# Grouped-query attention on one core: in the one load queue, K of a step behind V of two steps back, V singly

## The chip, the cores and the metric

The kernel runs on one core of one Trainium2 chip. The metric is the device time of one execution in microseconds (us), lower being better. A core has several engines that each take their own instruction stream in order: TensorE (PE, the matmuls; PEld is its loading of the stationary operand), VectorE (DVE), ScalarE (ACT), GpSimd (POOL) and SyncE (SP), which here does nothing but issue data transfers (DMAs). Engines tell each other by semaphores when a piece of work is done, and a DMA raises a semaphore when it has landed.

## What is computed

Two independent problems, A and B, of the same shapes; their results are put side by side in the output. Of each:

```python
# x [16, 80, 576], k_cache and v_cache [16, 16, 512, 128], wq [576, 4096], wo [4096, 576], all bf16
q = (x @ wq).reshape(B, Sq, Hq, Dh).transpose(0, 2, 1, 3)       # 32 query heads of 128
k = jnp.repeat(k_cache, rep, axis=1)                            # 16 KV heads, each for rep = 2 query heads
v = jnp.repeat(v_cache, rep, axis=1)
scores = jnp.einsum("bhqd,bhkd->bhqk", q, k) * (Dh ** -0.5)
p = softmax(scores, axis=-1)
o = jnp.einsum("bhqk,bhkd->bhqd", p, v)
return o.transpose(0, 2, 1, 3).reshape(B, Sq, Hq * Dh) @ wo
```

## The kernel before

**Tiling.** The attention goes in 128 steps `U`, 64 for each problem. A step is one batch element with four KV heads (so eight query heads): its K is one tile of 128 x 4 x 512 bf16 (512 KB), its V another. Eight steps with the same four heads form an octet; for an octet the queries are projected first (`qp`, line 599, and the copy out of PSUM, 615 and 617). Per step, with keys on the partitions:

- 16 score blocks of 128 keys by 160 (two heads of 80 queries), line 714. They run through all steps in groups of three, `qk0`, `qk1`, ..., so that group `t` holds blocks 3t to 3t + 2, and step `U` begins with block 16U.
- For each group the maximum of every row over its three blocks (line 720, DVE) and the exponential (line 724, ACT).
- As every row of a group has a maximum of its own, V's rows have to be scaled to make up for it: a common minimum (744, 747, 751), weights `wt` (754, ACT), and on POOL a cast (757, `wc`) and six multiplications of V by the weights (775, `vs`), whose result is `vp`.
- The products with `vp`: four of four matmuls (`pv`, line 800) and the rest of the queries for a pair of steps (`pr`, 819); then the division by the sums (836, 841, 846), the transposes (863) and their copies (875, 877).

The output projection (`op`, 968) follows in pieces of 16 matmuls, over half the heads at a time; its sums stay in `acc` and go out through four buffers `osb` (996, stores 1002).

PE takes the scores of a step some two steps ahead of its products, so K of a step is used about two steps ahead of V of the same step.

**Buffers.** `kT` has five buffers for K (`NK`), `v_sb` four for V (`NV`). K of step `U` may be loaded when the scores of step `U - 5` are done, V of step `U` when POOL has done the six multiplications of step `U - 4`; both are semaphore waits of SP.

**The queue.** Nearly all loads and the stores are issued by SP, in one order. K is loaded by a transposing DMA (`ldk`, line 682), V by a plain copy (`ldv`, 686); between them stand the pieces of wq (570, 573), wo (645), the transposed x of problem B (537) and the stores (1002). SP issues them strictly in order: while one waits for its buffer, all behind it wait.

**The planner.** The orders of all engines are made while the program is built. `_Sched` is told every operation with a key (where it would stand), what it reads and writes, an assumed duration and a stream, walks through an assumed time and gives each engine the operation that is ready and has the lowest key. `after` names a mark (a number, where mark 4U + u is the product `pv` of step U, head u, or the name of an operation): the operation isn't placed before that one has been. It is a matter of the order alone; at run time there are only the semaphore waits that follow from `reads` and `writes`. What the lines touched by the change do before:

- `KPH = 35`, `KU0 = 10`: from step 10 on, K of step `U` is placed after mark 4U - 35.
- `KRD`: from step 10 on K goes in pairs: that of an even step also waits for the buffer of the next one (resource `kd`, written by every score group).
- `VPH = 16`, `VU0 = 14`: from step 14 on V is placed 2 us (`VLAG`) after mark 4U - 16, the first product of step U - 4.
- `VRD`: from step 14 on V goes in pairs: that of an even step also waits for the buffer of the next one (resource `vd`, written by the last multiplication of every step).
- `VPE`: V of steps 4, 5, 6 and 7 is placed after marks 8, 11, 14 and 17.

The order that comes out in the middle, for instance: K 26, K 27, V 24, V 25, K 28, K 29, V 26, V 27, with weights and stores between.

Of the kernel before, what the change touches and what calls it, by code (L numbers as in the profile page):

```python
# [14 lines left out]
NV = 4  # L15
# [7 lines left out]
VK = 14.0  # L23
# [18 lines left out]
FKEY = dict([(n_, i_ - 100.0) for i_, n_ in enumerate(FIRST)] + [(n_, 0.05 * i_ - 0.49) for i_, n_ in enumerate(LATER)])  # L42
LAND = dict(x00=4.1, w00=6.4, x01=8.0, w01=9.6, k0=11.5, w10=14.5, k1=16.0, v0=18.3, k2=20.5, v1=22.5, k3=25.2, k4=28.0, v2=30.5, k5=33.8, x10=35.4, x11=36.4, w11=39.0, v3=40.6, k6=43.2)
# [5 lines left out]
VENG = "sp"  # L49
# [1 line left out]
VLAG = 2.0  # L51
VPH = 16
VU0 = 14
VPE = {4: 8, 5: 11, 6: 14, 7: 17}
KPH = 35
KU0 = 10
KLAG = 0.0
# [6 lines left out]
NVS = 4  # L64
# [302 lines left out]
def bass_concat_heads__gqa_block_cached__gqa_block_cached__near_ridge_kernel(  # L367
# [18 lines left out]
    NSU = 2 * UPR  # L386
# [8 lines left out]
    with ExitStack() as es:  # L395
# [9 lines left out]
        vp = sb("vp", [128, NVP, 18, VW], BF16)  # L405
# [31 lines left out]
        S = _Sched()  # L437

        def R(res, ver):
            return (res, ver)  # L440
# [37 lines left out]
        def em_warmend(e):  # L478
# [5 lines left out]
              stream="warmset")  # L484
# [12 lines left out]
        for half in range(NPP):  # L497
            x_ap = probs[0][0]
            for part, (k0, k1) in enumerate(XP):
                def em_ldx(e, x_ap=x_ap, half=half, k0=k0, k1=k1):  # L500
# [5 lines left out]
                      writes=[R(("xs", half * NRT + k_), 0) for k_ in range(k0, k1)], dsem="d_x%d%d" % (half, part), land=LAND["x%d%d" % (half, part)],  # L506
                      name="ldx%d.%d" % (half, part), stream="first", dur=0.5, cost=XC * (k1 - k0))
            for blk in range(NRT):
# [11 lines left out]
                def em_xev(e, en=None, half=half, blk=blk, vb=vb):  # L520
# [4 lines left out]
                      stream="X", dur=_mm(5, 128), lat=0.2, alloc=[vb])  # L525
                S.add(("act", "dve") if half else "act" if blk in (1, 3) else "dve", x + 0.3, em_xev, reads=[R(vb, 0)], writes=[R(("xT", half, blk), 0)],
                      name="xev%d" % rb, stream="xed" if half else "xea" if rb in (1, 3) else "xev",
                      dur=dict(act=0.52, dve=0.40), lat=0.13)

        for half in range(NPP):  # L530
            x_ap = probs[1][0]
            st0 = UPR + 16 * half - lead[NG // 2 + 2 * half]
            for ck in range(5):
                def em_ldxt(e, x_ap=x_ap, half=half, ck=ck):
# [6 lines left out]
                      writes=[R(("xT", half, b_), 1) for b_ in range(NRT)] if ck == 0 else [R(("xT", half, "t", ck), 1)],  # L541
                      dsem="d_x%d0" % half, name="ldxt%d.%d" % (half, ck), stream="x", dur=0.7, cost=0.85, xp=True,
                      after=int(4 * (st0 + XR[half][0] + XR[half][1] * ck)))
# [5 lines left out]
        for goct in range(NG):  # L549
# [6 lines left out]
            for pi, (c0, c1) in enumerate(pieces):  # L556
# [10 lines left out]
                for j, (k0, k1, n0, n1) in enumerate(parts):  # L567
                    def em_ldw(e, wq_ap=wq_ap, q=q, wsl=wsl, n0=n0, n1=n1, k0=k0, k1=k1):
                        if k0 == 4:
# [7 lines left out]
                          writes=[R(("wq", wsl, w_, p_), wv) for w_ in range(k0, k1) for p_ in range(n0 // 256, n1 // 256)],  # L577
                          dsem="d_we%d_%d_%d" % (goct, pi, j) if goct < 2 else "%s_%d" % (dsem, j),
                          name="ldw%d.%d.%d.%d" % (goct, pi, k0, n0), stream="wqa" if not goct + pi + j else strm if goct < 2 or k0 < 4 else "wqb", dur=0.5,
                          cost=((0.12 + 0.8 * WQC) * (k1 - k0) / 4.0 if k0 < 4 else 0.4) * (n1 - n0) / 1024.0 * (1.0 if goct < 2 or k0 == 4 else 0.96),  # L580
                          after=int(4 * (sp_ + at)) if goct > 1 else None,
                          lag=WLAG if goct > 1 else 0.0,
                          land=LAND["w%d%d" % (goct, pi)] if goct < 2 else 0.0)

            for i in range(8):
                for c in range(2):
# [34 lines left out]
                    if prob:  # L621
                        xr += [R(("xT", half, "t", ck), 1) for ck in range(1, 5)]
                    S.add("pe", x, em_qp,
                          reads=[R(("wq", wsl, w_, i // 2), wv) for w_ in range(5)] + [R(("wqz",), 0)] + xr,
                          writes=[R(vb, 0)] + [R(("qT", qpos(goct, bl), i), goct) for bl in range(b0, b0 + nb)],
                          name="qp%d.%d.%d" % (goct, i, c), stream="Q" if goct else "Q0",
                          dur=_mm(5, n1 - n0), lat=0.2, alloc=[vb])
                    S.add(("act", "dve"), x + 0.4, em_qev, reads=[R(vb, 0)],
                          writes=[R(("qT", qpos(goct, bl), i), goct) for bl in range(b0, b0 + nb)],
                          name="qev%d.%d.%d" % (goct, i, c), stream="qev" if goct else "qev0",  # L630
                          dur=QEV[n1 - n0] if qpos(goct, b0) + nb <= NQS else QEV[n1 - n0, 2])

        for sg in range(2 * NPAIR):
# [4 lines left out]
            for n in range(2 * NWC):  # L638
# [4 lines left out]
                def em_ldwo(e, wo_ap=wo_ap, h0=h0, hc=hc, wc=wc, c3=c3):  # L643
# [7 lines left out]
                      writes=[R(("wo", c3, wc), sg)]  # L651
                      + ([R(("warm",), 3 + c3), R(("ones",), 1 + c3)] if sg == 0 and wc == 0 else []),
                      dsem="d_wo%d" % c3, name="ldwo%d.%d.%d" % (sg, c3, wc), stream="wo", dur=0.5, cost=WOC,
                      after=int(4 * (base + w0 + ws_ * wc)), lag=WLAG)
# [2 lines left out]
        NT = (NBK + 2) // 3  # L657
        PT0 = [16 * U // 3 for U in range(NSU)]

        def VRD(U):  # L660
            if U < VU0 or U % 2 or U + 1 >= NSU:
                return []
            return [R(("vd", U + 1 - NV), 0)]

        def KRD(U):
            if U < KU0 or U % 2 or U + 1 >= NSU:
# [6 lines left out]
        for U in range(NSU):  # L673
            goct, bl = divmod(U, 8)
            prob, q, half = unit(goct)
            b = half * 8 + bl
            _, kc_ap, vc_ap, _, _ = probs[prob]
            ks, vs = U % NK, U % NV

            def em_ldk(e, kc_ap=kc_ap, b=b, q=q, ks=ks):  # L680
                src = kc_ap[b, 4 * q:4 * q + 4, :, :].rearrange("g (p j) d -> (g p) j d", j=4)
                return e.dma_start_transpose(kT[:, ks, :, :], src)

            def em_ldv(e, vc_ap=vc_ap, b=b, q=q, vs=vs):
                src = vc_ap[b, 4 * q:4 * q + 4, :, :].rearrange("g (p j) d -> p g (j d)", j=4)
                return e.dma_start(v_sb[:, vs, :, :], src)

            S.add("sp", FKEY["k%d" % U] if U < NFK else 5.0 * U - LA - KK, em_ldk, reads=KRD(U), writes=[R(("kT", ks), U)],
                  dsem="d_k%d" % ks, name="ldk%d" % U, stream="K" if U >= NFK else "first", dur=1.8, cost=KC, xp=True,
                  after=4 * U - KPH if U >= KU0 else None, lag=KLAG if U >= KU0 else 0.0, land=LAND.get("k%d" % U, 0.0))  # L690
            S.add(VENG if U >= NVS else "sp", FKEY["v%d" % U] if U < NVS else 5.0 * U - VK, em_ldv, reads=VRD(U),
                  writes=[R(("V", vs), U)],
                  dsem="d_v%d" % vs, name="ldv%d" % U, stream="V" if U >= NVS else "first", dur=VDUR, cost=VC,
                  lag=VLAG if U >= NVS else 0.0, after=VAF[U] if U < 4 else 4 * U - VPH if U >= VU0 else VPE.get(U),
                  land=LAND.get("v%d" % U, 0.0))

        for t in range(NT):
            blks = []
            for B_ in range(3 * t, min(3 * t + 3, NBK)):
                U, r_ = divmod(B_, 16)  # L700
# [22 lines left out]
            def em_exp(e, vb=vb, si=si, sl=sl, n=n):  # L723
# [5 lines left out]
                  name="max%d" % t, stream="max", dur=0.045 + n * 0.00108, lat=0.12, ahead=MXO)  # L729
            S.add("act", kq(t) + 1.1, em_exp, reads=[R(vb, 0), R(("nm", si), t)], writes=[R(("P", sl), t)],  # L730
                  name="exp%d" % t, stream="exp", dur=0.045 + n * 0.00106, lat=0.2)

        for U in range(NSU):
            goct, bl = divmod(U, 8)
            prob, q, half = unit(goct)
            vr, vs, gs = U % NV, U % NVP, U % 2
# [19 lines left out]
            def em_wc(e, gs=gs, vs=vs):  # L756
# [4 lines left out]
                  writes=[R(("gm", gs), U)], name="g%d" % U, stream="g", dur=0.07, lat=0.13, ahead=RCO)  # L761
            S.add("pe", kg + 1.1, em_mb, reads=[R(("gm", gs), U), IDENT], writes=[R(vbx, 0)], name="mb%d" % U,
                  stream="G", dur=_mm(1, 128), lat=0.2, alloc=[vbx], ahead=RCO)
# [3 lines left out]
                  writes=[R(("w", gs), U)], name="w%d" % U, stream="w", dur=0.195, lat=0.15, ahead=RCO + 2.0)  # L767
            S.add("pool", kg + 1.45, em_wc, reads=[R(("w", gs), U)], writes=[R(("vp", vs, "c"), U)], name="wc%d" % U,
                  stream="vs", dur=0.167, lat=0.1)
            for r in range(6):  # L770
                p0, p1 = max(3 * r, off), min(3 * r + 3, off + 16)

                def em_vs(e, p0=p0, p1=p1, vr=vr, vs=vs, off=off, gs=gs, r=r):
                    src = v_sb[:, vr, :, :].rearrange("p g (j d) -> p (g j) d", d=128)[:, p0 - off:p1 - off, :]
                    return e.tensor_scalar(vp[:, vs, p0:p1, 0:128], src, wt[:, gs, r:r + 1], 1.0,  # L775
                                           op0=AluOpType.mult, op1=AluOpType.mult)

                S.add("pool", kg + 1.5 + 0.5 * r, em_vs, reads=[R(("w", gs), U), R(("V", vr), U)],
                      writes=[R(("vp", vs, r), U)] + ([R(("vd", U), 0)] if r == 5 else []), name="vs%d.%d" % (U, r), stream="vs",
                      dur=0.241 + 0.107 * (p1 - p0), lat=0.1)  # L780

            if U % 2 == 0:
# [9 lines left out]
            for u in range(4):  # L792
# [3 lines left out]
                def em_pv(e, u=u, vo=vo, c0=c0, vs=vs, where=where):  # L796
# [10 lines left out]
                    reads=[R(("P", (t0 + r_) % NPS), t0 + r_) for r_ in rs_] + [R(("vp", vs, r_), U) for r_ in rs_ + ["c"]],  # L807
# [23 lines left out]
            for h_, (a_, b_, xo) in enumerate(((0, 3, 2.5), (3, 6, 6.5), (6, 8, 8.5), (8, 10, 9.2))):  # L831
# [6 lines left out]
                def em_on(e, en, pi=pi, vo=vo, a_=a_, b_=b_):  # L838
# [6 lines left out]
                    for k in range(a_, b_):  # L845
# [5 lines left out]
                      stream="rcp", dur=0.08, lat=0.13, ahead=RCO)  # L851
# [364 lines left out]
```

## Time and profile before

| | us |
|---|---|
| three runs: median (lowest to highest) | 721.7 (720.84 to 724.67) |
| the profiled execution: its own time | 718.9 |
| the profiled execution: its span, first to last instruction | 717.1 |

TensorE's granted clock was 0.997 over that execution. All the views that follow are of it; its times are counted from the start of the span. A row of a group reads: line, engine, operation, tile written <- tiles read, shapes, count | busy us, mean ns of one | idle us of the engine just before them, and what ended it. A row of a wait reads: who <- whom: us in total, times, longest us. A row of the timeline reads: start us, us, engine, line, operation, tiles, count [idle us before <- what ended it]. SP's rows (SPq) tell how long it was held by an issue; when a DMA landed is told apart, as "DMA to landing", counted from the start of its issue.

### The profile page before, as it was taken

The page shows a single profiled execution, that of the slowest core. Times are in us where ns is not written, and L with a number is a line of the kernel's source. Part 1 is how long each engine was busy: PE and PEld are TensorE (multiplying, and loading weights), DVE is VectorE, ACT ScalarE, POOL GpSimd, SP SyncE. Part 2 cuts the span into 40 slices and gives each one's busy share as a digit, 9 for nine tenths or more (in the row PEclk, how much of TensorE's full clock was granted, in tenths as well). Part 3 has the DMA queues.
Part 4 walks back from the last instruction along what each step waited for, and adds up shares of the span by engine and source line. Part 5 has one row for each costly group of instructions (what it writes and reads, how often), then busy time and mean ns, then how long its engine had stood idle before and what let it go on. Part 6 is the DMA issues. An engine that isn't in the chain of part 4 may idle for free.

```text
span 717.1 us, 23699 instructions
## 1 busy us (share of the span) xinstructions
PE 696.7 (97%) x9533; PEld 582.2 (81%) x9533; DVE 625.7 (87%) x1605; ACT 588.7 (82%) x1307; POOL 432.5 (60%) x904
## 2 busy tenths in 40 slices
PE   8989999999999999999999999999899999999997
PEld 5658888888888888777888888888788888888885
DVE  5979999998898998988899899899799989999982
ACT  2868988799999899778879888888888889988960
POOL 1546766657567665747556666666566575757570
PEclk9999999999999999999999999999999999999999
DMA  9999999999999999999999999999999988999921
GB/s 234 238 228 259 236 227 261 236 217 244 227 220 232 232 238 245 235 248 230 232 233 225 219 247 234 255 252 211 242 226 208 217 207 226 251 222 241 221 77 33
DMA packets 371028, 160.77 MB, mean 224 GB/s; under 512 B 276832, under 2 KB 367456, under 8 KB 370912
## 3 DMA queue, kind: packets, MB, share of 16 engines
q1 hardware_dynamic: 370832, 159.12, 102.4%
q8 instruction: 77, 1.26, 0.7%
q14 instruction: 39, 0.32, 0.2%
q10 hardware_dynamic: 80, 0.07, 0.0%
HBM read 87.46 MB, written 2.95 MB: 126 GB/s over the span
## 4 chain that ended last, share of the span: by engine, by line
PE 72%; DVE 8%; DMA 8%; POOL 6%; ACT 5%; issue 1%; SPq 1%
PE ps L599 18%; PE ps L968 18%; PE ps L714 14%; PE ps L800 12%; DMA v_sb<-in_A_v_cache_dram 6%; POOL vp L775 6%; DVE negmax L720 5%; PE ps L863 4%; PE ps L819 4%; ACT p_sb L724 3%; DMA v_sb<-in_B_v_cache_dram 1%; PE ps L747 1%; DVE qT L617 1%; PE ps L471 1%; ACT o_sb L846 1%
## 5 line engine op out<-in xcount | busy, mean ns | idle before, releaser
L724 ACT ACTIVATE p_sb<-ps,negmax 128x480 bf16<-128x480 f32 (+1 forms) x683 | 427.3, 679 | 55.0 <-DVE negmax L720 51.3
L775 POOL TENSOR_SCALAR vp<-v_sb,wt 128x384 bf16<-128x384 bf16 (+2 forms) x768 | 407.8, 552 | 41.0 <-DMA v_sb<-in_A_v_cache_dram 32.8
L720 DVE TENSOR_REDUCE negmax<-ps 128x1 f32<-128x480 f32 (+1 forms) x683 | 418.4, 647 | 13.1 <-PE ps L714 11.9
L714 PE MATMUL ps<-qT,kT 128*128 128x160 bf16 x2048 | 233.0, 232 | 1.1 <-ACT p_sb L724 0.7
L599 PE MATMUL ps<-xT,wq_sb 128*128 128x320 bf16 (+2 forms) x1280 | 213.6, 300 | 1.2 <-DVE xT L521 0.6
L800 PE MATMUL ps<-vp,p_sb 128*128 128x129 bf16 x2048 | 195.0, 221 | 10.5 <-POOL vp L775 8.1
L714 PEld LDWEIGHTS ps<-qT,kT 128*128 128x128 bf16 x2048 | 154.1, 97 | 19.1 <-ACT p_sb L724 2.9
L757 POOL CAST vp<-wt 128x18 bf16<-128x18 f32 x128 | 33.8, 264 | 222.8 <-ACT wt L754 222.4
L800 PEld LDWEIGHTS ps<-vp,p_sb 128*128 128x128 bf16 x2048 | 141.8, 98 | 22.5 <-issue 3.6
L599 PEld LDWEIGHTS ps<-xT,wq_sb 128*128 128x128 bf16 x1280 | 115.6, 98 | 35.7 <-DVE wo_sb L479 1.1
L968 PE MATMUL ps<-wo_sb,oTe 128*128 128x288 bf16 x640 | 91.5, 286 | 0.3 <-DVE gmn L751 0.3
L968 PE MATMUL ps<-wo_sb,oTo 128*128 128x288 bf16 x640 | 91.5, 286 | 0.0
L846 ACT ACTIVATE o_sb<-ps,rinv 128x128 bf16<-128x128 f32 x255 | 77.8, 393 | 4.7 <-DVE rinv L836 3.8
L841 DVE TENSOR_TENSOR o_sb<-ps,rinv 128x384 bf16<-128x384 f32 (+1 forms) x155 | 74.7, 484 | 2.0
L617 DVE TENSOR_SCALAR qT<-ps 128x320 bf16<-128x320 f32 (+2 forms) x125 | 59.7, 480 | 16.2 <-PE ps L599 15.7
L968 PEld LDWEIGHTS ps<-wo_sb,oTo 128*128 128x128 bf16 x640 | 60.6, 98 | 13.8
L968 PEld LDWEIGHTS ps<-wo_sb,oTe 128*128 128x128 bf16 x640 | 59.8, 98 | 13.7 <-DVE gmn L751 0.7
L615 ACT ACTIVATE qT<-ps 128x320 bf16<-128x320 f32 (+1 forms) x131 | 57.9, 443 | 12.2 <-PE ps L599 12.1
L863 PE MATMUL ps<-ident,o_sb 128*128 128x128 bf16 x640 | 49.0, 220 | 0.0
L836 DVE RECIPROCAL rinv<-ps 128x3 f32<-128x3 f32 (+1 forms) x256 | 41.1, 167 | 9.0 <-PE ps L819 5.7
L754 ACT ACTIVATE wt<-negmax,gmn 128x6 f32<-128x6 f32 x128 | 40.9, 320 | 7.8 <-DVE gmn L751 7.3
L751 DVE TENSOR_REDUCE gmn<-ps 128x1 f32<-128x128 f32 x128 | 36.4, 284 | 9.4 <-PE ps L747 9.3
(37 smaller groups left out, 310.4 us busy)
## 6 DMA issues: line engine op xcount, KB each, us to landing
v_sb<-in_A_v_cache_dram SPq DMA_DIRECT2D x64, 512.0 KB, 5.3
v_sb<-in_B_v_cache_dram SPq DMA_DIRECT2D x64, 512.0 KB, 5.4
wo_sb<-in_A_wo_dram SPq DMA_DIRECT2D x16, 288.0 KB, 5.9
wo_sb<-in_B_wo_dram SPq DMA_DIRECT2D x16, 288.0 KB, 6.1
wq_sb<-in_B_wq_dram SPq DMA_DIRECT2D x16, 256.0 KB, 4.8
out_dram<-osb SPq DMA_DIRECT2D x40, 72.0 KB, 4.0
wq_sb<-in_A_wq_dram SPq DMA_DIRECT2D x4, 512.0 KB, 5.2
wq_sb<-in_A_wq_dram SPq DMA_DIRECT2D x8, 256.0 KB, 5.5
```

The source lines that it names most:

```text
L599: last = e.matmul(ps[:, vb.phys, 0:n1 - n0], lhsT=wq_sb[:, wsl, ck, i * 128:(i + 1) * 128], rhs=xT[:, half, ck, n0:n1], start=(ck == 0), s ...
L615: r_ = e.activation(dst, src[:, s0:s0 + n_, :], AF.Identity, scale=SCALE)
L617: r_ = e.tensor_scalar(dst, src[:, s0:s0 + n_, :], SCALE, None, op0=AluOpType.mult)
L714: last = e.matmul(ps[:, vb.phys, i * 160:(i + 1) * 160], lhsT=kT[:, U % NK, j, u * 128:(u + 1) * 128], rhs=qT[:, qpos(U // 8, U % 8), u * ...
L720: return e.tensor_reduce(negmax[:, si:si + 1], ps[:, vb.phys, 0:n], axis=AX.X, op=AluOpType.max, negate=True)
L724: return e.activation(p_sb[:, sl, 0:n], ps[:, vb.phys, 0:n], AF.Exp, bias=negmax[:, si:si + 1], scale=1.0)
L775: return e.tensor_scalar(vp[:, vs, p0:p1, 0:128], src, wt[:, gs, r:r + 1], 1.0, op0=AluOpType.mult, op1=AluOpType.mult)
L800: last = e.matmul(ps[:, vo.phys, c0:c0 + 129], lhsT=p_sb[:, sl, i * 160:i * 160 + 128], rhs=vp[:, vs, p_, 0:129], start=(j == 0), stop=(j ...
L841: return e.tensor_tensor(o_sb[:, pi % NOS, a_:b_, :], src[:, :, 0:128], rinv[:, pi % NRI, a_:b_].unsqueeze(2).broadcast_to([128, b_ - a_, ...
L846: last = e.activation(o_sb[:, pi % NOS, k, :], src[:, k - a_, 0:128], AF.Identity, scale=rinv[:, pi % NRI, k:k + 1])
L863: last = e.transpose(dst, o_sb[:, pi % NOS, 4 * h2 + k if k < 4 else 8 + h2, :], ident[:])
L968: last = e.matmul(ps[:, vb.phys, 0:DC], lhsT=lhsT, rhs=wo_sb[:, hi, c3 * DC:(c3 + 1) * DC], start=(hi == 0), stop=(hi == HH - 1))
```

## The change

`VPE` is emptied. `VRD` and the resource `vd` go, so that every V waits for its own buffer only. `KAF` takes the place of the mark for K: from step 6 on K of step `U` is placed after V of step U - 2; from step 10 on the two of a pair are both placed after V of the step before the pair, that is, an even K after V of step U - 1 and an odd one after V of step U - 2. `KRD` stays. `VPH` and `VLAG` stay for V from step 14 on.

```diff
-VPE = {4: 8, 5: 11, 6: 14, 7: 17}
+VPE = {}
...
-        def VRD(U):
-            if U < VU0 or U % 2 or U + 1 >= NSU:
-                return []
-            return [R(("vd", U + 1 - NV), 0)]
+        def KAF(U):
+            if U < 6:
+                return None
+            return "ldv%d" % min(U - 2 + (U >= KU0 and U % 2 == 0), NSU - 1)
...
             S.add("sp", FKEY["k%d" % U] if U < NFK else 5.0 * U - LA - KK, em_ldk, reads=KRD(U), writes=[R(("kT", ks), U)],
                   dsem="d_k%d" % ks, name="ldk%d" % U, stream="K" if U >= NFK else "first", dur=1.8, cost=KC, xp=True,
-                  after=4 * U - KPH if U >= KU0 else None, lag=KLAG if U >= KU0 else 0.0, land=LAND.get("k%d" % U, 0.0))
-            S.add(VENG if U >= NVS else "sp", FKEY["v%d" % U] if U < NVS else 5.0 * U - VK, em_ldv, reads=VRD(U),
+                  after=KAF(U), lag=0.0, land=LAND.get("k%d" % U, 0.0))
+            S.add(VENG if U >= NVS else "sp", FKEY["v%d" % U] if U < NVS else 5.0 * U - VK, em_ldv,
                   writes=[R(("V", vs), U)],
...
-                      writes=[R(("vp", vs, r), U)] + ([R(("vd", U), 0)] if r == 5 else []), name="vs%d.%d" % (U, r), stream="vs",
+                      writes=[R(("vp", vs, r), U)], name="vs%d.%d" % (U, r), stream="vs",
```

The order that comes out for the steps above: V 24, V 25, K 26, K 27, V 26, V 27, K 28, K 29, each V with a wait of its own. In the start-up: V 3, V 4, K 6, V 5, K 7, V 6, K 8, V 7, K 9, V 8, V 9, K 10, K 11 (before: V 3, K 6, K 7, K 8, V 4, K 9, V 5, V 6, V 7, V 8, K 10, V 9, K 11). On POOL the order is the same as before; on PE, DVE and ACT it differs at one place, where the chain of the minimum and the weights of step 18 (744, 747, 751, 754) stands behind one more output projection piece (16 matmuls of line 968) and the two instructions of a query projection and a score group have changed places.

## Prediction

> **What bounds the kernel now.** I read the page first: TensorE (PE) is busy almost throughout, so only its idle time, 717.1 - 696.7 = 20.4 us, is to be had from a change of order.
>
> ```profile
> span 717.1 us, 23699 instructions
> PE 696.7 (97%) x9533; PEld 582.2 (81%) x9533; DVE 625.7 (87%) x1605; ACT 588.7 (82%) x1307; POOL 432.5 (60%) x904
> DMA  9999999999999999999999999999999988999921
> ```
>
> The third row says that the DMA engines are occupied to the end of the loads: a transfer that goes earlier pushes another back. Next, the stretches: where is PE idle?
>
> ```profile
> 0.00:60.00 60.00, 53.60 (x547) 37.89 (x548) 43.81 (x106) 35.21 (x71) 22.77 (x50) 0.97 1.06 243
> 95.00:165.00 70.00, 69.21 (x971) 58.06 (x972) 64.91 (x167) 60.02 (x135) 45.76 (x96) 1.00 1.10 244
> 270.00:375.00 105.00, 100.81 (x1384) 84.80 (x1382) 93.00 (x239) 85.60 (x184) 64.09 (x133) 1.00 1.15 236
> 440.00:512.00 72.00, 69.45 (x980) 58.62 (x979) 61.87 (x160) 62.13 (x142) 45.59 (x95) 1.00 1.08 236
> 512.00:690.00 178.00, 177.32 (x2508) 151.60 (x2506) 164.53 (x426) 157.57 (x352) 114.67 (x240) 1.00 1.00 220
> ```
>
> The columns are the stretch, its length, the busy us of PE, PEld, DVE, ACT and POOL, granted clock, DMA share, GB/s. PE idles 6.4 us in the first 60, 0.8, 4.2 and 2.6 in the next three, and 0.7 in the last, where the DMA engines moved 220 GB/s instead of 236 to 244. The last is loose; the three before it I call crowded. Next, who PE waits for, over the whole span (first row) and in the stretches (0 to 60, 60 to 270, 270 to 375, 440 to 512):
>
> ```profile
> L800 PE MATMUL ps<-vp,p_sb 128*128 128x129 bf16 x2048 | 195.0, 221 | 10.5 <-POOL vp L775 8.1 <-ACT p_sb L724 2.1
> POOL vp L775 <- DMA v_sb<-in_A_v_cache_dram: 32.8, 14, 6.5
> PE ps L800 <- POOL vp L775: 2.9, 1, 2.9
> PE ps L800 <- POOL vp L775: 0.7, 2, 0.4
> PE ps L800 <- POOL vp L775: 3.9, 6, 1.4
> PE ps L800 <- POOL vp L775: 0.6, 1, 0.6
> PE ps L800 <- ACT p_sb L724: 1.9, 1, 1.9
> 505.99 3.18 POOL L775 TENSOR_SCALAR vp<-v_sb,wt 128x384 bf16<-128x384 bf16 x6 [2.85 <-DMA v_sb<-in_B_v_cache_dram]
> 507.28 0.39 PE L800 MATMUL ps<-vp,p_sb 128*128 128x129 bf16 x4 [1.89 <-ACT p_sb L724]
> ```
>
> The chain is one: V lands late, POOL's scaling (L775) starts late, and the V product (L800) holds PE. The 1.9 us put down to ACT are of it too: POOL began that step at 505.99, after 2.85 us of waiting for V, and two of its six slices (3.18 / 6 x 2 = 1.06) end at 507.05, just before PE goes on at 507.28. V's lateness so costs 8.1 + 2.1 = 10.2 us: 2.9 in the start-up, 7.3 later.
>
> **The change part by part.** No instruction is added or removed; in the built program POOL's order is the same, and PE, DVE and ACT differ at one place. SP's queue changes throughout, and POOL's semaphore is waited for by 123 V loads instead of 64.
>
> *V of steps 4 to 7.* Before, V of step 4 stands behind K of 6, 7 and 8:
>
> ```profile
> 33.12 0.51 SPq L686 DMA_DIRECT2D v_sb<-in_A_v_cache_dram  x1
> 33.67 10.50 SPq L682 DMA_TRANSPOSE kT<-in_A_k_cache_dram  x3
> 44.22 0.60 SPq L686 DMA_DIRECT2D v_sb<-in_A_v_cache_dram  x1
> 42.84 0.27 POOL L757 CAST vp<-wt 128x18 bf16<-128x18 f32 x1 [0.47 <-ACT wt L754]
> 49.65 3.18 POOL L775 TENSOR_SCALAR vp<-v_sb,wt 128x256 bf16<-128x256 bf16 x6 [6.54 <-DMA v_sb<-in_A_v_cache_dram]
> 50.84 0.39 PE L800 MATMUL ps<-vp,p_sb 128*128 128x129 bf16 x4 [2.92 <-POOL vp L775]
> DMA to landing us min/median/max: 4.5/6.0/8.8
> L714 PE MATMUL ps<-qT,kT x97: 230/232/243, 12.4 to 47.3; 128*128 128x160 bf16 x97
> ```
>
> After, it goes at 33.7 instead of 44.22, and lands some 10.5 us earlier, by about 39.2 (POOL's start at 49.65, less 10.5); the weights are ready at 42.84 + 0.27 = 43.1, so POOL starts there and PE's 2.9 us go. What is late next: K of step 6 now goes 0.6 us later, plus at most 2.0 for the V in front (half of the 3.9 found below for two). By the longest landing of this stretch, 8.8, it is there at 33.7 + 8.8 + 2.6 = 45.1; its first matmul (the 97th of L714, six steps of 16 being done) is at 47.3. Covered: **-2.9**.
>
> *K behind V, and V singly.* A crowded pair of steps before, in SP's queue, and on POOL:
>
> ```profile
> 293.13 1.06 SPq L686 DMA_DIRECT2D v_sb<-in_A_v_cache_dram  x2
> 295.44 8.45 SPq L682 DMA_TRANSPOSE kT<-in_A_k_cache_dram  x2
> 304.56 0.98 SPq L686 DMA_DIRECT2D v_sb<-in_A_v_cache_dram  x2
> 286.95 3.18 POOL L775 TENSOR_SCALAR vp<-v_sb,wt 128x128 bf16<-128x128 bf16 x6 [0.52 <-DMA v_sb<-in_A_v_cache_dram]
> 291.07 3.18 POOL L775 TENSOR_SCALAR vp<-v_sb,wt 128x384 bf16<-128x384 bf16 x6
> 310.19 3.18 POOL L775 TENSOR_SCALAR vp<-v_sb,wt 128x384 bf16<-128x384 bf16 x6 [3.93 <-DMA v_sb<-in_A_v_cache_dram]
> DMA to landing us min/median/max: 4.5/6.9/8.7
> ```
>
> These are V of 52 and 53, K of 56 and 57, V of 54 and 55. The buffers of V 54 and 55 come free when POOL has done steps 50 and 51, at 286.95 + 3.18 = 290.1 and 294.3, yet V is asked for at 304.56: 14 and 10 us late. After, both go as soon as the queue has them, ahead of K 56, by about 295, 10 us earlier; POOL waited 3.93 us there, so V would be some 6 us early. The price is K's. SP takes the queue in order, so a V that waits holds K, weights and stores behind it. K 56 lands by 295.44 + 8.7 = 304.1, and K 66, asked for at 353.45, by 353.45 + 6.9 = 360.4 (the longest and the median of the stretch):
>
> ```profile
> 353.45 6.66 SPq L682 DMA_TRANSPOSE kT<-in_B_k_cache_dram  x2
> L714 PE MATMUL ps<-qT,kT x897: 230/232/243, 12.4 to 309.0; 128*128 128x160 bf16 x180
> L714 PE MATMUL ps<-qT,kT x1057: 230/232/243, 12.4 to 364.4; 128*128 128x160 bf16 x177
> 543.84 4.52 SPq L682 DMA_TRANSPOSE kT<-in_B_k_cache_dram  x2
> ```
>
> Their first matmuls, the 897th and 1057th, are at 309.0 and 364.4: 4.9 and 4.0 us in reserve. What two V in front cost a K, no row shows. Low end: their issue alone, 1.06. High end: a pair of K takes SP 8.45 us here, behind a burst, and 4.52 in the loose stretch, so 3.9. I take 3.9, as the engines are full here. Of K's reserve 1.0 and 0.1 are then left, while PE would like to be 4.1 us earlier (3.9 of that stretch and 0.2 under ACT's name). So V's wait is half exchanged for one on K. From both ends: nothing of the 7.3 comes back, or all. By stretch I take 0 of 0.7 before 270; 1.5 of 4.1 in 270 to 375 (about 1 up to K 66, the rest behind it); and 2.0 of 2.5 after 440, most of it the single wait at 507: **-3.5**.
>
> The Trainium skill, "DMA: Bandwidth & Descriptors", section "Anatomy of one DMA — SWDGE (gpsimd) path", says that DMA engines do not wait on semaphores, the issuing sequencer does. That speaks against the change, as each V now waits at SP's head. The same page's "Latency and other measured facts" gives 261 GB/s for transposing DMAs, from which I estimate 2.0 us for a K of 512 KB; the trace has 4.52 for two in the loose stretch, but 8.45 in the crowded one. By the page's rate K would never be late and all 10.2 us would come back (the second rival).
>
> *The rest.* The one moved compute place delays the weights of step 18 by two half output projections, 16 matmuls of 91.5 / 640 = 0.14 us, 2.3 us:
>
> ```profile
> L968 PE MATMUL ps<-wo_sb,oTo 128*128 128x288 bf16 x640 | 91.5, 286 | 0.0
> 120.97 3.19 POOL L775 TENSOR_SCALAR vp<-v_sb,wt 128x384 bf16<-128x384 bf16 x6 [2.87 <-DMA v_sb<-in_A_v_cache_dram]
> ```
>
> POOL waited 2.87 us for V of that step, with its weights there, which covers it: 0, or 2.3 at most without the cover. In the loose stretch nothing waits on V or K: 0.
>
> Sum: -2.9 - 3.5 = -6.4 on a span of 717.1. The profiled execution took 718.9, the median of the three runs is 721.7; the span's change carries over, so 721.7 - 6.4 = **715.3**.
>
> **The rivals.** *An exchange*: K takes V's place as what PE waits for in every crowded stretch, for the whole 7.3. For it: reserves of 4.0 and 4.9 against a price of 3.9, and full engines. Against it: some of the waits come after the tightest K. Only -2.9 is left: 718.8. *All of it back*: the price of V is nearer 1.06 than 3.9, so K stays in reserve: 721.7 - 10.2 = 711.5. Against it: the three crowded stretches, at 236 to 244 GB/s, have no room that any row shows. *Slower*: transposes and copies are mixed more. In the built queue a transpose stands behind a copy 93 times, before 81. A K right behind a copy took SP 3.21 us, against 4.52 / 2 = 2.26 for one of a loose pair:
>
> ```profile
> 278.48 0.58 SPq L573 DMA_DIRECT2D wq_sb<-in_B_wq_dram  x1
> 279.10 3.21 SPq L682 DMA_TRANSPOSE kT<-in_A_k_cache_dram  x1
> ```
>
> If the 12 more cost 0.95 each, all in crowded stretches, SP's queue falls back 11.4 us; once K's reserve is gone, each shows on PE, while K takes V's 7.3: 721.7 - 2.9 + 11.4 = 730.2. Against it: the new neighbours are mostly stores, the smallest transfers. That V would not come earlier I leave out: the order gives it.
>
> **How the numbers follow.** Forecast 0.32, exchange 0.24, all back 0.18, slower 0.26. A change under 0.5%, 3.6 us, can't be told from none. Faster by more holds 0.30 of the forecast, all of "all back" and 0.02 of the exchange: 0.50. Slower is 0.26; the rest, 0.02 of the forecast and 0.22 of the exchange, is no change: 0.24. The range reaches from 2 us below "all back", 709.5, over the exchange to 726, half of the way from there to "slower", which leaves out its dearer half and little else; the forecast's own is 712 to 718.
>
> **What would show it.** Right: POOL's idle before L775 no longer names V (32.8 us before), the 2.9 us before the V product at 50.8 are gone, and PE's idle shrinks to about 14 us, with small waits on K at L714 in 95 to 165 and 270 to 375. Wrong: waits of several us at L714 for K, growing over 270 to 375 (slower); the gap at 50.8 still there; or SP's pairs of K taking longer than 8.45 with PE's idle as before (exchange).

## The result, and the profile after

| | before | after |
|---|---|---|
| median (lowest to highest), us | 721.32 (712.88 to 725.02, 12 runs) | 727.18 (724.44 to 730.64, 12 runs) |
| ratio after / before, 95% interval | | 1.011 (1.0074 to 1.0146) |
| the profiled execution: its own time, its span, us | 718.9, 717.1 | 724.44, 722.7 |

The change made the kernel 1.1% slower. The forecast was 715.3 us, the range 709.5 to 726.

First the page of the changed kernel.

```profile
span 722.7 us, 23697 instructions
PE 697.6 (97%) x9533; PEld 584.0 (81%) x9533; DVE 626.3 (87%) x1605; ACT 589.9 (82%) x1307; POOL 429.0 (59%) x904
```

PE idles 722.7 - 697.6 = 25.1 us, before 20.4. Of the 5.6 us that the span grew, 4.7 are idle time. Next the waits over the whole span of the changed kernel (who <- whom: us, times, longest).

```profile
PE ps L714 <- DMA kT<-in_A_k_cache_dram: 12.3, 7, 2.9
POOL vp L775 <- DMA v_sb<-in_A_v_cache_dram: 2.8, 1, 2.8
PE ps L714 <- DMA kT<-in_B_k_cache_dram: 1.9, 2, 1.6
SPq L686 <- POOL vp L775: 50.9, 68, 4.3
```

And one row of the kernel before, from the same view:

```profile
SPq L686 <- POOL vp L775: 20.4, 45, 1.4
```

Nearly the whole of V's lateness is gone: POOL waits for V once, 2.8 us in the start-up, where it waited 32.8 us for V of problem A alone, and no wait of PE for `vp` is left in the view. In its place stands a wait that was not there before: PE waits 12.3 + 1.9 = 14.2 us for K at L714. That is 4.0 more than the 10.2 which V cost.

The two rows of SP have to be read with care. They count from the end of SP's previous issue to the last signal that POOL gave before this issue ended, also where V's buffer had been free long before. Worked out from the ends of POOL's multiplications and from SP's own rows, V of the changed kernel really stood for its buffer 16 times, some 31 us in all; before, twice and 0.8 us. Of the 31 us, 30 fall into 165 to 270 and 512 to 690, and none into 95 to 165, 270 to 375 or 440 to 512. In return K no longer stands for its own buffer, which it did 25 times and some 66 us before. The longest of V's waits, of the changed kernel: two V in one row, of which the second goes out when POOL is done, at 198.97 + 3.17 = 202.14.

```profile
197.25 5.28 SPq L686 DMA_DIRECT2D v_sb<-in_A_v_cache_dram  x2
198.97 3.17 POOL L775 TENSOR_SCALAR vp<-v_sb,wt 128x384 bf16<-128x384 bf16 x6
```

Next, where PE loses: the stretches of the changed kernel (columns as in the prediction).

```profile
0.00:60.00 60.00, 56.33 (x630) 41.10 (x631) 48.66 (x120) 39.59 (x84) 25.89 (x58) 1.00 1.04 243
60.00:95.00 35.00, 32.51 (x445) 26.24 (x442) 30.76 (x79) 31.60 (x74) 20.74 (x45) 0.95 1.14 230
95.00:165.00 70.00, 67.56 (x958) 57.10 (x957) 63.56 (x163) 59.16 (x132) 45.92 (x96) 1.00 1.09 246
270.00:375.00 105.00, 96.25 (x1304) 80.62 (x1302) 86.36 (x222) 81.21 (x175) 59.42 (x125) 0.97 1.10 230
440.00:512.00 72.00, 70.12 (x992) 59.65 (x990) 64.17 (x164) 62.43 (x140) 44.87 (x95) 1.00 1.10 240
512.00:690.00 178.00, 177.61 (x2512) 151.96 (x2510) 162.87 (x421) 157.61 (x355) 114.95 (x242) 1.00 1.02 226
```

and the one stretch of the kernel before that the prediction did not show:

```profile
60.00:95.00 35.00, 34.49 (x515) 28.59 (x513) 33.86 (x90) 34.27 (x82) 23.41 (x49) 1.00 1.12 226
```

The counts in brackets after PE's busy time are its instructions, so they tell how far the program has come (one that runs across a boundary is counted on both sides, so the sums are a few too high). By 60 us the changed kernel is 630 - 547 = 83 matmuls ahead: the start-up gain is real. By 165 us it has done 630 + 445 + 958 = 2033, and the kernel before 547 + 515 + 971 = 2033: nothing of the gain is left. In 270 to 375 it does 1304 instead of 1384 and idles 8.75 us instead of 4.19. In 440 to 512 it is a little better than before, in the loose stretch equal.

One K, close up. That of step 50 was the first of a crowded stretch in both kernels. Its first matmul is the 801st of L714. Before: the queue, the time from issue to landing of that one transfer, and the row of the matmuls up to its use.

```profile
262.74 3.81 SPq L682 DMA_TRANSPOSE kT<-in_A_k_cache_dram  x1
DMA to landing us min/median/max: 5.7/5.7/5.7
L714 PE MATMUL ps<-qT,kT x801: 230/232/243, 12.4 to 275.6; 128*128 128x160 bf16 x161
```

After: the same, and PE's row where it is used.

```profile
268.90 0.58 SPq L686 DMA_DIRECT2D v_sb<-in_A_v_cache_dram  x1
269.53 6.67 SPq L682 DMA_TRANSPOSE kT<-in_A_k_cache_dram  x1
DMA to landing us min/median/max: 9.0/9.0/9.0
278.69 0.56 PE L714 MATMUL ps<-qT,kT 128*128 128x160 bf16 x3 [2.94 <-DMA kT<-in_A_k_cache_dram]
```

Before, it landed at 262.74 + 5.7 = 268.4, 7.2 us before its use at 275.6. After, it goes out 6.8 us later. In the queue five more transfers stand ahead of it than before: V of steps 48 and 49, two pieces of wq and one of the transposed x. It then takes 3.3 us longer (9.0), and lands at 278.5: 10.1 us later in all. Its reserve of 7.2 is used up and PE waits 2.94. Neither this K nor a V ahead of it in this stretch stood for its buffer.

The two V alone are most of it. K of step 48 has only two V more ahead of it than before, and no weights or x. It went out 5.1 us later and landed 5.4 us later (after its issue it took 8.3 us before and 8.6 after):

```profile
250.92 5.71 SPq L682 DMA_TRANSPOSE kT<-in_A_k_cache_dram  x1
256.02 8.00 SPq L682 DMA_TRANSPOSE kT<-in_A_k_cache_dram  x2
```

The first row is of the kernel before, the second of the changed one, there merged with K of step 49. My estimate from the rate of the changed kernel in 270 to 375, 230 GB/s: two V of 512 KB take 4.6 us.

Over the steps 48 to 65, K landed a median of 6.8 us before its first matmul before the change and 1.5 after it; V landed 1.6 us before its first multiplication on POOL before, and 6.3 after (each worked out from landings and first uses, as for step 50, of those tiles whose landing the trace tells). So the reserve was moved from K, which has the earlier use, to V.

### The profile page after: what moved, and what is told of

It is laid out like the page before. It is cut to its first block, busy times and chain, and to the rows that moved or that the text cites. A ratio compares the mean times of both kernels' runs of the same rounds, so it can differ in the third digit from the quotient of the medians.

```text
span 722.7 us, 23697 instructions
## 1 busy us (share of the span) xinstructions
PE 697.6 (97%) x9533; PEld 584.0 (81%) x9533; DVE 626.3 (87%) x1605; ACT 589.9 (82%) x1307; POOL 429.0 (59%) x904
## 3 DMA queue, kind: packets, MB, share of 16 engines
q8 instruction: 78, 1.28, 0.8%
## 4 chain that ended last, share of the span: by engine, by line
PE 77%; DMA 12%; DVE 8%; ACT 2%; issue 0%; SPq 0%
PE ps L968 20%; PE ps L599 19%; PE ps L714 16%; PE ps L800 12%; DMA kT<-in_A_k_cache_dram 9%; DVE negmax L720 5%; PE ps L819 4%; PE ps L863 4%; DMA kT<-in_B_k_cache_dram 2%; ACT p_sb L724 1%; PE ps L747 1%; DVE qT L617 1%; DVE o_sb L841 1%; PE ps L471 0%; ACT o_sb L846 0%
## 5 line engine op out<-in xcount | busy, mean ns | idle before, releaser
L714 PE MATMUL ps<-qT,kT 128*128 128x160 bf16 x2048 | 234.1, 233 | 16.2 <-DMA kT<-in_A_k_cache_dram 12.3
L714 PEld LDWEIGHTS ps<-qT,kT 128*128 128x128 bf16 x2048 | 154.7, 97 | 35.8 <-issue 9.9
L968 PE MATMUL ps<-wo_sb,oTo 128*128 128x288 bf16 x640 | 93.0, 289 | 0.0
L819 PE MATMUL ps<-vp,p_sb 128*32 128x129 bf16 x2048 | 42.8, 226 | 0.6 <-ACT o_sb L846 0.6
```

The costliest lines, as they stand in the source:

```text
L714: last = e.matmul(ps[:, vb.phys, i * 160:(i + 1) * 160], lhsT=kT[:, U % NK, j, u * 128:(u + 1) * 128], rhs=qT[:, qpos(U // 8, U % 8), u * ...
L819: last = e.matmul(ps[32 * u:32 * u + 32, od.phys, 129 * h_:129 * h_ + 129], lhsT=p_sb[:, sl, i * 160 + 128:i * 160 + 160], rhs=vp[:, vs_, ...
L968: last = e.matmul(ps[:, vb.phys, 0:DC], lhsT=lhsT, rhs=wo_sb[:, hi, c3 * DC:(c3 + 1) * DC], start=(hi == 0), stop=(hi == HH - 1))
```

## The experiments

To sort the kernels I count how many steps K stands ahead of V in SP's queue: the step of a K less the step of the last V in front of it, the mean over steps 14 to 125. The kernel before has 3.5, the changed kernel 1.5. PE uses K about two steps ahead of V of the same step.

Theory A: K's place behind V takes its reserve, and PE waits for K instead of V. Theory B: the new mixture of transposes and copies slows the transfers. Theory C: a V that waits alone at the head of SP's queue is what costs.

**The start-up alone.**

```diff
-VPE = {4: 8, 5: 11, 6: 14, 7: 17}
+VPE = {}
```

> Only V of steps 4 to 7 is asked for as its buffers come free; K and the pairs of V as before. Theory A (K's reserve: in the crowded stretches K, put behind two V and the weights between them, lands too late, while V gets more lead than it can use): the start-up gain stays, 2 to 5 us faster than before, and no wait on K at L714 over 1 us. Theory B (mixing: the queue itself takes longer, as transposes and copies alternate more often; here 82 times against 81): as before within 0.3% but for the same start-up gain. Theory C (head of the queue: SP idles behind a V that waits singly): as A.

Measured: 721.16 us, ratio 1.001 (0.9975 to 1.0045). PE's waits for `vp`, and the first stretches, of this kernel:

```profile
PE ps L800 <- POOL vp L775: 12.0, 13, 2.6
0.00:60.00 60.00, 56.52 (x626) 40.99 (x627) 48.35 (x120) 39.32 (x83) 25.98 (x57) 1.00 1.06 243
60.00:95.00 35.00, 34.46 (x487) 28.45 (x485) 33.72 (x86) 34.78 (x82) 23.57 (x50) 1.00 1.12 230
95.00:165.00 70.00, 66.16 (x939) 55.42 (x937) 61.40 (x157) 56.25 (x127) 43.61 (x90) 1.00 1.10 246
```

By 60 us this kernel is 79 matmuls ahead of the one before, by 165 us 626 + 487 + 939 = 2052, only 19 ahead. In 95 to 165 PE idles 3.84 us instead of 0.79: the gain waits there for loads. It is real at its place, and the 2 to 5 us that were expected of it at the end did not come.

**V singly alone** (no `VRD`, no `vd`; `VPE` and K's mark as before).

```diff
-            S.add(VENG if U >= NVS else "sp", FKEY["v%d" % U] if U < NVS else 5.0 * U - VK, em_ldv, reads=VRD(U),
+            S.add(VENG if U >= NVS else "sp", FKEY["v%d" % U] if U < NVS else 5.0 * U - VK, em_ldv,
...
-                      writes=[R(("vp", vs, r), U)] + ([R(("vd", U), 0)] if r == 5 else []), name="vs%d.%d" % (U, r), stream="vs",
+                      writes=[R(("vp", vs, r), U)], name="vs%d.%d" % (U, r), stream="vs",
```

> Only V singly; K by its mark and the start-up as before. The order becomes K 32, V 31, K 33, V 32 and the like, and a transpose stands behind a copy 104 times (before 81, after the change 93). A: V's waits on POOL shrink, K loses only about one V's worth of reserve: 0 to 5 us faster than before. B: slower than the changed kernel, 730 or more. C: 3 to 6 us slower than before, with SP's waits for POOL at L686 at about 50 us.

Measured: 722.2 us, ratio 1.0014 (0.9979 to 1.0049), with a transpose right behind a copy 104 times. That speaks against B. Of C it is hardly a test: the row of SP's waits for POOL has 28.9 us here instead of the 50 expected, and by the ends of POOL's multiplications V stood for its buffer only some 4 us. The gain that A allowed is not to be seen either.

**K behind V alone** (`VPE` and the pairs of V as before).

```diff
+        def KAF(U):
+            if U < 6:
+                return None
+            return "ldv%d" % min(U - 2 + (U >= KU0 and U % 2 == 0), NSU - 1)
...
-                  after=4 * U - KPH if U >= KU0 else None, lag=KLAG if U >= KU0 else 0.0, land=LAND.get("k%d" % U, 0.0))
+                  after=KAF(U), lag=0.0, land=LAND.get("k%d" % U, 0.0))
```

> Only K behind V of two steps back; V still in pairs from step 14 on, so that SP waits for POOL half as often (the order begins V 3, V 4, K 6 here too, since K's place frees V's). A: K late as in the changed kernel, 725 to 730, 10 us or more of waits on K at L714. B: 96 alternations, 727 to 730. C: 722 or less, as the single waits are gone.

Measured: 735.38 us, ratio 1.023 (1.0181 to 1.0279). PE's largest waits (L719 is line 714 of the others, five lines lower):

```profile
PE ps L719 <- DMA kT<-in_A_k_cache_dram: 10.5, 7, 3.0
PE ps L719 <- DMA kT<-in_B_k_cache_dram: 10.5, 6, 2.8
```

21.0 us on K. This one edit makes the loss, and with V in pairs it is dearer than in the changed kernel. Here no V from step 14 on goes alone, and the loss is there all the same, so theory C falls as it was put. V's waits are not gone, though: some 27 us, worked out as above, and none of them in 95 to 165, 270 to 375 or 440 to 512. So a pair's wait hardly explains the further 1.2%; what does stays open.

**Both edits of V, K's mark as before.**

```diff
-VPE = {4: 8, 5: 11, 6: 14, 7: 17}
+VPE = {}
...
-            S.add(VENG if U >= NVS else "sp", FKEY["v%d" % U] if U < NVS else 5.0 * U - VK, em_ldv, reads=VRD(U),
+            S.add(VENG if U >= NVS else "sp", FKEY["v%d" % U] if U < NVS else 5.0 * U - VK, em_ldv,
```

> The whole change but for K's place: V singly and V of steps 4 to 7 as the buffers come free, K by its mark. 105 alternations. A: faster than before by 3 to 8 us, 713 to 718, no single wait on K over 2 us. B: slower than the changed kernel, 730 or more. C: like the changed kernel, 725 to 729.

Measured: 720.23 us, ratio 0.9997 (0.9964 to 1.003).

```profile
PE ps L800 <- POOL vp L775: 7.1, 9, 1.5
PE ps L714 <- DMA kT<-in_B_k_cache_dram: 2.4, 3, 1.3
```

With 2.5 steps between K and V, both are waited for a little (7.1 us, 2.4, and 1.0 for K of problem A), for about as long together as V alone before. So the 3 to 8 us that theory A hoped for here did not come. But without K's new place the loss is gone. A transpose stands right behind a copy 105 times, more often than in the changed kernel (93), without loss: theory B falls.

**Where the loss is made.** The profile points to 270 to 375. So K behind V only for the steps loaded there, and the complement, everything else as in the changed kernel:

```diff
-                  after=KAF(U), lag=0.0, land=LAND.get("k%d" % U, 0.0))
+                  after=KAF(U) if 46 <= U < 74 else 4 * U - KPH if U >= KU0 else None, lag=0.0, land=LAND.get("k%d" % U, 0.0))
```

> The changed kernel, but K goes behind V of two steps back for steps 46 to 73 alone (loaded in the crowded stretch of 270 to 375 us); all other K are placed by the mark of before. In the queue K then stands 1.5 steps ahead of V in those steps and 2.4 to 2.6 in the others (before 3.5 throughout, changed kernel 1.5 throughout). Theory A (K's place behind V makes K late, and it costs where the engines of the loads are full): PE waits for K by several us within 270 to 375 as in the changed kernel, 10 to 14 us over the span, most of it there; ratio 1.003 to 1.012, 723.5 to 730 us. Theory B (the order outside that stretch, or the start-up, or V singly, makes the loss): ratio within 0.998 to 1.003.

> The complement: the changed kernel, but K of steps 46 to 73 placed by the mark of before (2.5 steps ahead of V), all others behind V of two steps back (1.5 steps ahead). Theory A with the loss in the crowded stretch of 270 to 375 us alone: no wait on K there, ratio 0.996 to 1.003. If every crowded stretch pays its share: waits on K before 165 and in 440 to 512 of 1 to 3 us each, ratio 1.002 to 1.007. If the loss has nothing to do with K's place there: 1.008 to 1.014 as in the changed kernel.

Measured: the middle alone 721.27 us, ratio 1.0004 (0.9971 to 1.0036); the rest alone 725.64 us, ratio 1.0072 (1.0043 to 1.0102). The waits on K of problem A, in this order:

```profile
PE ps L714 <- DMA kT<-in_A_k_cache_dram: 6.3, 6, 2.9
```

```profile
PE ps L714 <- DMA kT<-in_A_k_cache_dram: 7.7, 6, 2.4
```

The reading of one profile was wrong here. The middle brings waits on K (4.5 us of the 6.3 in 270 to 375), but no loss that shows, against what theory A expected of it; most of the loss comes from the other steps. So the rest was cut once more, with the same line and the conditions `U < 46` and `U >= 74`.

> The changed kernel with K behind V of two steps back only up to step 45 (loaded in the first 250 us); from step 46 on K by the mark of before. The complement of the middle cost 0.72% (0.43 to 1.02), the middle alone 0.04% (-0.29 to 0.36). If the loss is made before 165 us, in the start-up and the crowded stretch behind it: ratio 1.004 to 1.009, waits on K there of 5 us or more. If it is made behind 375 us: 0.997 to 1.003. If both give a share: 1.002 to 1.005.

> The changed kernel with K behind V of two steps back only from step 74 on (loaded after about 390 us); before that K by the mark. If the loss is made before 165 us: ratio 0.997 to 1.003. If it is made behind 375 us: 1.004 to 1.009, with waits on K of 3 us or more in 440 to 512. If both give a share: 1.002 to 1.005.

Measured: the early steps 723.2 us, ratio 1.0034 (1.0005 to 1.0062); the late ones 724.47 us, ratio 1.0027 (1.0003 to 1.0051). Each gives a share that is just clear of zero, together 0.61% against the 0.72% of the complement. The waits on K are 4.2 us before 165 in the early one, a little less than expected, and 3.2 us in 440 to 512 in the late one. The early part in its stretches 0 to 95 and 95 to 165:

```profile
0.00:95.00 95.00, 85.84 (x1047) 65.19 (x1048) 76.36 (x189) 68.46 (x150) 45.93 (x99) 0.98 1.08 232
95.00:165.00 70.00, 67.42 (x928) 56.54 (x925) 64.54 (x166) 59.81 (x132) 44.43 (x94) 1.00 1.09 240
```

By 165 us it has done 1975 matmuls, 58 fewer than the kernel before. That alone does not show where its time went: V singly alone, without a loss in the median, was as far back in its profile (1041 by 95 us and 933 more by 165). The medians show that K's place costs in more than one part of the program; one profile of each kernel cannot show in which stretch an execution loses it.

**K one step later still.**

```diff
-            return "ldv%d" % min(U - 2 + (U >= KU0 and U % 2 == 0), NSU - 1)
+            return "ldv%d" % min(U - 2 + (U >= KU0) + (U >= KU0 and U % 2 == 0), NSU - 1)
```

> The changed kernel with K one step later still: from step 10 on an even K behind V of its own step, an odd K behind V of the step before, so K stands 0.5 steps ahead of V in the queue instead of 1.5. Theory A: V of a step waits for its buffer and holds K behind it, K has no reserve left anywhere; PE waits for K in most pairs of steps, 20 to 60 us in all, V never; 740 to 780 us, ratio 1.025 to 1.08. Rival (mixing of transposes and copies, of which this queue has the fewest, a transpose standing right behind a copy 86 times against 93 in the changed kernel and 81 before): not slower than the changed kernel, ratio 1.00 to 1.01.

Measured: 747.8 us, ratio 1.0401 (1.0339 to 1.0462).

```profile
PE 704.8 (95%) x9533; PEld 580.4 (78%) x9533; DVE 649.4 (87%) x1655; ACT 570.6 (77%) x1240; POOL 427.9 (58%) x904
PE ps L714 <- DMA kT<-in_A_k_cache_dram: 13.3, 11, 2.3
PE ps L714 <- DMA kT<-in_B_k_cache_dram: 1.9, 4, 0.8
```

As theory A has it in time, and the opposite of what the mixture (86 times against 93 in the changed kernel) would give. But PE's waits named K are 15.2 us, below the 20 to 60 expected, of an idle time of 743.1 - 704.8 = 38.3. The planner, which reckons with late K too, here shared the copies between DVE (1655 instead of 1605) and ACT in another way, so this time is not K's lateness alone.

**K between** (both edits of V, and K behind V one step earlier at the odd ones).

```diff
-            return "ldv%d" % min(U - 2 + (U >= KU0 and U % 2 == 0), NSU - 1)
+            return "ldv%d" % min(U - 2 - (U >= KU0 and U % 2), NSU - 1)
```

> V singly, no marks for V of steps 4 to 7, and K by the rule of the change but half a step to a step earlier: from step 10 on an even K behind V of two steps back, an odd K behind V of three steps back, so K stands 2.2 to 2.4 steps ahead of V (changed kernel 1.5, before 3.5; K is used about two steps ahead of V). A transpose stands right behind a copy 104 times. Theory A, with a threshold near the two steps by which K is used earlier: small waits on both K and V, some 10 us in all, none over 2 us; ratio 0.995 to 1.002. A loss in proportion to the steps by which K is moved back (1.1% for two): 1.006. Mixing: 1.01 or more.

Measured: 721.18 us, ratio 0.9998 (0.9963 to 1.0033). PE waits 11.3 us for K here and 2.9 for V, one of them 2.3 long, a little over what was expected, and yet there is no loss in the median.

| steps by which K stands ahead of V | kernels | ratio to before |
|---|---|---|
| 3.5 | start-up alone | 1.001 |
| 2.5 | V singly; both edits of V | 1.0014; 0.9997 |
| 2.3 | K between | 0.9998 |
| 1.5 | changed kernel; K behind V alone | 1.011; 1.023 |
| 0.5 | K one step later still | 1.040 |

These points look like a threshold and not like one slope. Down to a little over two steps, the distance by which PE uses K ahead of V, the median shows no difference; below it the kernels are slower, and the more so the further back K stands. The place is not all: two kernels at 1.5 differ by 1.2%, and the last row holds another sharing of the copies too. Nor do K's waits in one profile follow the loss: K between has 11.3 + 2.9 = 14.2 us of waits, as many as the changed kernel, and over steps 48 to 65 its K landed a median of only 0.7 us before use.

**What takes K's reserve: V's bytes, or V's waits?** In the changed kernel and in the one before, only half of V is loaded from step 14 on.

```diff
-            def em_ldv(e, vc_ap=vc_ap, b=b, q=q, vs=vs):
-                src = vc_ap[b, 4 * q:4 * q + 4, :, :].rearrange("g (p j) d -> p g (j d)", j=4)
-                return e.dma_start(v_sb[:, vs, :, :], src)
+            def em_ldv(e, vc_ap=vc_ap, b=b, q=q, vs=vs, gn=4 if U < VU0 else 2):
+                src = vc_ap[b, 4 * q:4 * q + gn, :, :].rearrange("g (p j) d -> p g (j d)", j=4)
+                return e.dma_start(v_sb[:, vs, 0:gn, :], src)
```

> The changed kernel, its order and all its waits, but from step 14 on only two of the four KV heads of V are loaded (256 KB instead of 512 KB; the other half of the buffer keeps what was there, so that part of the output differs). Theory A1 (K comes late because of the bytes of V that the load engines carry ahead of it): the waits on K after 95 us vanish, under 2 us in all; those of the start-up, before step 14, stay; ratio 0.980 to 0.992. Theory A2 (K comes late because a V that waits for its buffer at the head of SP's queue holds back the K behind it): V still waits there, 45 us or more in all, and PE still waits 8 us or more for K after 95 us; ratio 1.000 to 1.011.

> The kernel before with the same half of V from step 14 on. If the pace of the loads makes the waits of both kernels, the waits on V after 95 us (7.3 us) vanish here and the ratio is 0.983 to 0.993, within 0.004 of the changed kernel with half of V. If V's waits came from its late issue (its place behind K, and the pair's wait) and not from the engines, 3 us or more of them stay, ratio 0.994 to 1.000, slower than the changed kernel with half of V.

Measured: the changed order 708.43 us, ratio 0.9797 (0.9756 to 0.9837); the order of before 708.33 us, ratio 0.981 (0.9774 to 0.9847), both just below their expected ranges. The first four rows are of the changed order with half of V, its waits of SP for POOL behind 95 us and the three crowded stretches; the last is PE's wait for `vp` over the whole span of the order of before with half of V:

```profile
SPq L686 <- POOL vp L775: 99.9, 64, 6.3
95.00:165.00 70.00, 69.69 (x979) 58.65 (x978) 65.88 (x170) 61.20 (x137) 46.46 (x98) 1.00 1.09 211
270.00:375.00 105.00, 105.00 (x1478) 89.66 (x1475) 97.18 (x251) 90.18 (x198) 66.64 (x140) 1.00 1.00 196
440.00:512.00 72.00, 71.94 (x1013) 61.19 (x1011) 65.16 (x168) 63.60 (x142) 44.99 (x95) 1.00 0.99 207
PE ps L800 <- POOL vp L775: 2.8, 1, 2.8
```

V holds SP's queue for 99.9 us there (95 us by the ends of POOL's multiplications), some three times as long as the 30 of the changed kernel, and PE hardly idles: it is busy 105.00 us of 105 in the stretch where it idled 8.75. Only the waits on K of the start-up, where V is still whole, are left (3.9 us). So V's waits at the head of the queue make no loss by themselves, and fewer bytes take the loss away. As no V stood for its buffer in the three crowded stretches of the changed kernel, at 230 to 246 GB/s, it is the transfers ahead of K that make it late there. One thing is not shown: whether V's waits in 165 to 270, some 8 us, add to it by leaving the queue behind for the crowded stretch that follows; the core moved 221 GB/s in 165 to 270 instead of 228. In the order of before, the waits on V behind 95 us are gone with half of V too, and only the one of the start-up is left. Both orders come out equal, 0.1 us apart: with this much room in the load engines, the choice between them is worth nothing.

## Why the prediction was wrong

- **V of steps 4 to 7, -2.9: right at its place, wrong at the end.** The 2.9 us are gone, and the changed kernel and the start-up alone lead by some 80 matmuls at 60 us. But the sum carried them to the end as if nothing behind depended on the loads. Behind it, in 95 to 165, PE of the start-up alone idles 3.84 us instead of 0.79: it only comes to its next wait sooner. It is the same reason that the prediction gave for the late V, and left out for the early one.
- **K's price, 3.9 at most against a reserve of 4.9 and 4.0: the reserves were right, the price was too low.** K of step 56 and 66 had these reserves. This is the step of the sum that failed. Its upper bound for two V in front was the difference of a busy and a quiet pair of K, which is no row of a V at all; for K of step 48, with two V more ahead and nothing else, the price was 5.4. For K of step 50 it was 10.1, as pieces of wq and x had come ahead of it too (6.8 us later in the queue) and the transfer itself took 3.3 us longer. Over steps 48 to 65 the median reserve fell by 5.3, from 6.8 to 1.5. So the -3.5 became about +6.9: behind 60 us PE waits 14.2 us for K where it waited 7.3 for V. With the -2.9 of the start-up that is the +4.0 of above, and PE's idle time grew by 4.7.
- **The upper end of the range.** 726 is called half of the way from the exchange to "slower". Half of the way from 718.8 to 730.2 is 724.5; the measured 727.18 is above both.
- **"Exchange" and "slower".** The wait did change over from V to K, as the rival said, but for 14.2 us and not for the same 7.3. The rival that came out on the right side had the wrong mechanism for its price: no cost of the mixture of transposes and copies shows, since 104 and 105 such changes ran at 1.0014 and 0.9997.
- **The rule on the sequencer that waits** (the Trainium skill, "DMA: Bandwidth & Descriptors", section "Anatomy of one DMA — SWDGE (gpsimd) path"), which the prediction set against the change, agrees with the trace as to where V waits: SP stood some 31 us for V's buffers instead of 0.8. As a reason for the loss it isn't borne out: SP stood less for V and K together than before (31 us instead of 67), not at all for V in the stretches called crowded, and with half of V some 95 us without a loss.
- **The signs given.** POOL no longer waits for V but for 2.8 us, as foreseen; PE's idle time grew to 25.1 us instead of shrinking to 14; the waits of several us at L714 for K in 270 to 375 came, which the prediction named as the sign that it is wrong.
- **Left out: the clock.** The prediction has no term for it. Three waits on K were followed by a stretch at half clock; in the kernel before, one wait on V was. That is the next section but one.

What stays open: why the middle alone, and K between, cost nothing in the median, though K's reserve over steps 48 to 65 is as small there (median 1.4 and 0.7 us) as in the changed kernel (1.5); and why K behind V alone is dearer than the changed kernel.

## What to carry to other kernels

In one queue before full load engines, order transfers by when they are used: count by how many steps the consumer takes the one ahead of the other, and keep at least that distance in the queue (here a little over two). A wait that vanished in a stretch bound by its loads only moved to the next transfer here; fewer bytes gave it back (2% for half of V). Price a transfer that is moved back by the bytes that come to stand in front of it, over the rate of that stretch, the third parties too. Take a loss that one profile puts in a stretch for a sample until it is tried there alone. And before a row is read as a wait for a buffer, look whether the buffer was still in use.

## What the hardware showed beside it

After some waits of PE on K the granted clock fell to half for some us. The changed kernel, two windows of 3 us (the clock is the column before the DMA share), and the same eight matmuls of the output projection shortly before and in the second of them:

```profile
77.00:80.00 3.00, 3.00 (x18) 2.14 (x17) 1.81 (x5) 0.95 (x3) 2.21 (x5) 0.53 1.03 235
279.00:282.00 3.00, 3.00 (x42) 1.87 (x40) 1.25 (x4) 0.66 (x1) 1.05 (x3) 0.51 0.87 203
```

```profile
274.55 1.14 PE L968 MATMUL ps<-wo_sb,oTe 128*128 128x288 bf16 x8
279.05 2.12 PE L968 MATMUL ps<-wo_sb,oTo 128*128 128x288 bf16 x8
```

Each such window lasts 3.41 us and so costs up to 1.7. The changed kernel has three, behind waits of 2.09, 2.94 and 2.57 us; the kernel before has one, behind its 2.92; the start-up alone and both edits of V have none. A wait of 2.51 us in the changed kernel had none, nor had shorter ones there. In other kernels a wait of 2.63 us had none (the start-up alone), and one of 1.28 us had one (K behind V up to step 45, at 288 us), so no length that decides it shows. A wait of some 2 us can cost more than its length, and the two more windows are worth up to 3.4 us, of which a part falls where PE would have idled anyway: PE's busy time grew by 0.9 only. The Trainium skill, "TensorE: Matmul & The Clock Gate", section "What's actually happening", has a free-running window of 3413 ns and halves the clock after one idle window. The length agrees with the trace; but here waits shorter than the window were enough.
